# Attention scores as pairs of 64-row products, the first batch's values as pairs of 64-column products, and q and k without copies

## The chip, the cores and the metric

The kernel runs on one core of a Trainium2 chip. The metric is device time in microseconds (us) of one execution: the median of three runs before the change is 488.28 us (487.72 to 488.59).

## The reference, cut to what matters

Attention with a narrow local window and a few global keys, on 4 batches of 8 heads, 768 tokens and 64 values per head, is followed by a gated feed-forward block that mixes over tokens. Inputs and output are float32.

```python
scores = q @ k.T / 8 - slope[h] * dist          # per batch and head
keep   = (col < 8) | ((row - col >= 0) & (row - col < 96))
a      = softmax(where(keep, scores, -1e9))
x      = concat_heads(a @ v)                     # [4, 768, 512]
h      = relu(x @ w_in)                          # [4, 768, 1024]
u, vv  = h[..., :512], layer_norm(h[..., 512:])
out    = (u * (w_spatial @ vv + b)) @ w_out      # [4, 768, 512]
```

## The kernel before, in words

**Tiles.** The work is cut into 24 tiles of 128 tokens, six to a batch (n = 0 to 23, i = n mod 6). A query tile needs only its own block of 128 keys and the one before it, with the global keys copied over the first 32 columns of the older block. So the scores of a head are 128 rows by W columns, with W = 128 for i = 0 and 256 otherwise. `scores(n)` (line 942) makes them, adds the bias, takes the exponential and normalises. `values(n)` (line 1016) transposes them and multiplies with v. `mlp_v`, `mlp_u`, `mlp_s` and `mlp_o` (lines 1105 to 1181; V, U, G and O in the plan) are the feed-forward block; `setup_w_in`, `setup_w_out` and `setup_w_t` (I, Q and T, lines 815 to 828) split the weights into a high and a low part.

**Two ways of multiplying.** In the first batch (n < 6) q, k, v and the probabilities stay float32 (`whole_s`, `whole_v`); the trace shows each such product as two matrix instructions on TensorE (PE). In the other batches each operand is split into a high and a low part of a shorter format (fp32r) and one product is one instruction per pair of parts.

**Scores.** The array has 128 rows and one head fills 64. In the first batch q is stored twice with the other head's half zeroed (memsets at line 865), so that a product with all 128 rows of k gives one head (line 975): 8 products a tile. In the other batches q's high part is stored on both halves, and so is its low part; k's high part lies on the rows 0 to 63 and its low part on the rows 64 to 127. Two products of 128 rows (line 978) then sum all four pairs of parts: 16 products a tile. `split_qk` and `prep_k` (lines 891 to 905) load a block as `raw`, write the high part to `rawh` (ScalarE, ACT, mostly) and the low part back into `raw` (VectorE, DVE), and DMAs on SyncE's queue (SP) copy both into place: 8 of 128 KB for q (lines 879 to 882) and 4 for k. One pair of heads uses one PSUM bank.

**Values of the first batch.** v is stored with zero blocks between the heads (`padded`, line 926), so that a product of 128 columns fills the rows of one head and adds zero to the other's (lines 1049 to 1054): 16 products a tile, 8 for n = 0.

**Order.** All operations are first recorded (`Recorder`, line 89). `plan` (line 348) then simulates five queues with the durations of `cost` (line 223) and, for each engine, takes the ready operation of lowest rank; the ranks are the step's due time plus an offset in KEYS (line 534). Six PSUM banks are shared by scores (tag s), transposes (p), the feed-forward block (m) and the weights (cv); `room` (line 387) gives a bank to a new tile, and two more banks hold the results of `values`. `keep_warm` (line 505) puts spare transposes of the identity into gaps of PE in the first stretch. All operations are issued from line 39, which is why the profile shows that line everywhere.

Of the kernel before, what the change touches and what calls it, by code (L numbers as in the profile page):

```python
# [10 lines left out]
F32 = mybir.dt.float32  # L11
# [15 lines left out]
CFG = {'WS': 6, 'WV': 6, 'kept': 'p', 'bias1': 'pppppppp', 'bias2': 'a', 'S': [['I01', 'A'], ['I00', 'T00', 'T01', 'A', 'V00', 'B00'], ['T02', 'T03', 'A', 'V01', 'U00'], ['T04', 'T05', 'A', 'V02'], ['Q00', 'Q01', 'A', 'V03', 'U01'], ['Q02', 'Q03', 'A', 'V04']], 'T': [['V15', 'U12', 'A'], ['G10', 'O10', 'A'], ['G11', 'O11', 'A'], ['G12', 'O12', 'V00', 'V01', 'U00', 'A'], ['V02', 'A'], ['V03', 'U01', 'A', 'V04']], 'END': ['V05', 'U02', 'G00', 'O00', 'G01', 'O01', 'G02', 'O02'], 'whi': 'aaax', 'wsub': 'xx', 'wadd': 'v', 'wth': 'a', 'wtl': 'p', 'vhi': 'p', 'vlo': 'p', 'qhi': 'xv', 'qlo': 'v', 'khi': 'a', 'klo': 'v', 'pth0': 'a', 'x0h': 'x', 'x0l': 'v', 'pth': 'a', 'xh': 'aa', 'c1': 'a', 'xl': 'vppv', 'vnh': 'xvpa', 'vnl': 'p', 'gm': 'x', 'gh': 'aa', 'gl': 'x', 'o': 'vava', 'norm0': 'p', 'norm': 'p', 'wp': 3, 'wc': 'v', 'we': 'p',  'vrn': 'v', 'dup': 1, 'fold': '', 'xb': 1, 'div': 'v', 'rows': 'a', 'xf0h': 'aa', 'xf0l': 'pppp', 'xdiv': 'v', 'xbh': 'a', 'xbl': 'p', 'b_rawqk': 1, 'b_ev': 3, 'b_raw': 1, 'b_pr': 10, 'b_pth': 2, 'b_c1': 3, 'b_ps_s': 2, 'b_ps_p': 2, 'b_ps_o': 2, 'b_ps_m': 2}  # L27
# [3 lines left out]
class Op:  # L31
# [6 lines left out]
    def issue(self):  # L38
        getattr(self.real, self.call)(*[placed(x) for x in self.args], **{n: placed(x) for n, x in self.kw.items()})  # L39
# [49 lines left out]
class Recorder:  # L89
# [21 lines left out]

    def add(self, engine, call, args, kw):
        op = Op()
        op.ways = ((engine, call, args, kw),)
        op.token = self.now
        op.take(0)
        outs = [kw[x] for x in ("out", "accum_out") if x in kw]
        ins = [x for n, x in kw.items() if n not in ("out", "accum_out") and isinstance(x, (bass.AP, Ref))]
        aps = [x for x in args if isinstance(x, (bass.AP, Ref))]
        if "out" not in kw:  # L120
            outs.insert(0, aps.pop(0))
        op.writes, op.reads = outs, ins + aps
        op.num = len(self.ops)
        op.holds = list(dict.fromkeys(x.tile for x in outs + ins + aps if isinstance(x, Ref)))
        for v in op.holds:
            v.ops.append(op)
        self.ops.append(op)
# [95 lines left out]
def cost(op):  # L223

    out = op.writes[0]
    n = elements(out)
    src = op.reads[0] if op.reads else out
    psum = any(in_psum(x) for x in op.reads + op.writes[:1])
    parts = list(out.ap)[0][1]
    if op.eng == "tensor":  # L230
        if op.call == "transpose":
            return 109, 0, False
        n = elements(op.kw["rhs"])
        if op.kw["rhs"].dtype == F32:
# [24 lines left out]
    if op.call == "tensor_scalar" and not one and isinstance(op.kw.get("scalar1"), bass.AP) and n > 256:  # L259
        return 75 + .85 * n, 0, True  # L260
    if op.call in ("tensor_scalar", "tensor_copy") and not one:
        return (75 + 1.04 * n if out.dtype == I32 else 70 + .53 * n), 0, True
    if op.call in ("tensor_reduce", "bn_stats"):
        return 70 + 1.04 * elements(src), 0, False
    if op.call == "bn_aggr":
        return 180, 0, False
    return (190 if parts < P else 74) + 1.04 * n + (0 if one else 60), 0, not one


def link(ops):  # L270

    wrote, used, bank, forms = {}, {}, {}, {}
    for op in ops:
        preds = set()
        for ap in op.reads:
            name, p0, p1, bits = extent(ap)
            for q0, q1, b, o in wrote.get(name, ()):
                if q0 < p1 and p0 < q1 and b & bits:
                    preds.add(o)
        op.after = set(preds)  # L280
        for ap in op.reads + op.writes:

            own = ap.tile.name if isinstance(ap, Ref) else ap.tensor.name
            if own in places:
                mine = forms.setdefault(places[own], {})
                mine.setdefault(own, set()).add(op.num)
                for other in mine:
                    if other != own:
                        preds |= mine[other]
        for ap in op.writes:  # L290
            name, p0, p1, bits = extent(ap)
            for table in (wrote, used):
                for q0, q1, b, o in table.get(name, ()):
                    if q0 < p1 and p0 < q1 and b & bits:
                        preds.add(o)
        for ap in op.reads:
            name, p0, p1, bits = extent(ap)
            used.setdefault(name, []).append((p0, p1, bits, op.num))
        for ap in op.writes:
            name, p0, p1, bits = extent(ap)  # L300
            for table in (wrote, used):
                if name in table:
                    table[name] = [x for x in table[name] if not (p0 <= x[0] and x[1] <= p1 and x[2] | bits == bits)]
            wrote.setdefault(name, []).append((p0, p1, bits, op.num))
        if op.eng == "tensor":
            name = extent(op.writes[0])
            half = name[0], name[3].bit_length() > 1024
            if half in bank:
                preds.add(bank[half])
            bank[half] = op.num  # L310
# [22 lines left out]
def gates(ops):  # L333
# [3 lines left out]
    for v in {v: None for op in ops for v in op.holds}:  # L337
# [3 lines left out]
        if v.tag in IN_TURN:  # L341
            if v.tag in before:
                found.append((before[v.tag], first.num))
            before[v.tag] = first.num
# [3 lines left out]
def plan(ops, keys, trace=None):  # L348
# [38 lines left out]
    def room(x, e):  # L387

        v = ops[x].holds[0] if ops[x].holds else None
        if v is None or v.place is not None:  # L390
            return 0.0, None
        if len(banks) - 1 < sum(KEEP.get(tag, 0) for tag in FLOAT if tag != v.tag and not held[tag]):
            return None, None
        best = None
        for b, last in banks.items():
            at = max((reach(o, ops[x], e, ends[o.num], stands[o.num]) for o in last), default=0.0)
            if best is None or at < best[0]:
                best = at, b
        return best or (None, None)

    done = 0
    while done < n:
# [69 lines left out]
        done += 1  # L472
        for v in op.holds:
            if v.place is None:
                v.place = bank
                del banks[bank]
                held[v.tag] += 1
# [54 lines left out]
SLACK = 120  # L532
DMA_FIRST, DMA_PRE, DMA_POST, DMA_MARGIN = 4200.0, 800.0, 1400.0, 800.0
# [4 lines left out]
def attn_then_spatial_gating_kernel(  # L538
# [403 lines left out]
    def scores(n, qq):  # L942
# [25 lines left out]
        for g in range(NP):  # L968
            if g == 2:
                yield  # L970
# [398 lines left out]
```

## Time and profile before

| | |
|---|---|
| median of three runs | 488.28 us |
| the profiled execution's own time | 489.19 us |
| its span, first to last instruction | 487.4 us |
| granted clock of PE, mean | 0.998 |
| DMA traffic | 65.50 MB |

PE is TensorE's products, PEld its weight loads, DVE VectorE, ACT ScalarE, POOL GpSimd and SPq the queue of SyncE, which issues the DMAs. Products are pipelined: the duration of one is longer than the step from one to the next, so a step is read from the starts of two lines of the timeline, divided by the count of the first. Tiles are named by the program: `bank` is one of the six PSUM banks, `kring` and `q` are the operands of the scores, `ops` is the result of `values`, `vring` holds v, `pr` the probabilities, `pth` their transposes.

### The profile page before, as it was taken

What the parts mean: (1) busy time and instruction counts of PE and PEld (TensorE: products, weight loads), DVE (VectorE), ACT (ScalarE), POOL (GpSimd) and SP (SyncE); (2) the same over time, 40 slices, a digit from 0 to 9 for tenths busy, and PEclk for the clock granted to TensorE, in tenths of its full rate; (3) what the DMA queues carried; (4) which work ended last, traced back from release to release, by engine and by line L of the source; (5) the groups of instructions that cost most, each with busy time, mean ns of one, the idle gap of its engine ahead of it and who ended that gap; (6) DMA issues with size and microseconds to landing.
All of it is one profiled execution on the core that took longest, in us unless ns stands there. A gap on an engine that the chain in (4) does not pass through costs nothing.

```text
span 487.4 us, 10076 instructions
## 1 busy us (share of the span) xinstructions
PE 465.8 (96%) x3286; PEld 430.0 (88%) x3286; DVE 355.7 (73%) x1021; ACT 285.6 (59%) x773; POOL 267.4 (55%) x419
## 2 busy tenths in 40 slices
PE   7989999998999999899999999998989999999996
PEld 7778889998988779889999998998979998899995
DVE  3999788957686798798886787766766878762532
ACT  1899877653675577785745675665556576630112
POOL 4779897782363676687535263784243763543000
PEclk9999999999999999999999999999999999999999
DMA  6946634365645776665725552762564860000012
GB/s 208 319 155 179 179 114 114 99 155 141 154 116 164 204 191 176 169 166 139 199 68 150 153 151 86 197 173 66 133 154 118 220 166 25 34 1 3 22 45 71
DMA packets 38028, 65.50 MB, mean 134 GB/s; under 512 B 6000, under 2 KB 9840, under 8 KB 37968
## 3 DMA queue, kind: packets, MB, share of 16 engines
q1 hardware_dynamic: 37968, 64.77, 48.5%
q8 instruction: 28, 0.46, 0.4%
q14 instruction: 32, 0.26, 0.2%
HBM read 29.76 MB, written 6.68 MB: 75 GB/s over the span
## 4 chain that ended last, share of the span: by engine, by line
PE 60%; DMA 12%; DVE 10%; ACT 8%; issue 4%; SPq 3%; POOL 2%; DVEq 0%; ACTq 0%; POOLq 0%
PE bank L39 54%; PE ops L39 6%; ACT pr L39 4%; SPq L39 3%; DMA kring<-raw 3%; DVE pr L39 2%; DVE c L39 2%; DMA q<-raw 2%; DMA kring<-in_k_dram 2%; DMA raw<-in_k_dram 2%; DMA gl<-in_moe_w_spatial_dram 1%; DMA raw<-in_q_dram 1%; DVE bank L39 1%; ACT pth L39 1%; DMA gh<-in_moe_w_spatial_dram 1%
## 5 line engine op out<-in xcount | busy, mean ns | idle before, releaser
L39 POOL TENSOR_SCALAR pr<-pr,rc 128x256 f32<-128x256 f32 (+1 forms) x192 | 93.3, 504 | 27.4 <-DVE rc L39 13.9
L39 ACT ACTIVATE pr<-pr,mn 128x256 f32<-128x256 f32 (+1 forms) x192 | 92.1, 482 | 18.9 <-DVE mn L39 18.3
L39 DVE CUSTOM_DVE_ANT_0 pr<-bank,bias 128x256 f32<-128x256 f32 (+1 forms) x192 | 68.2, 396 | 12.5 <-PE bank L39 11.1
L39 PE MATMUL bank<-kring,q 128*128 128x256 f32 (+1 forms) x384 | 65.2, 304 | 6.2 <-DMA kring<-raw 2.1
L39 DVE TENSOR_TENSOR c<-ops,c 64x256 f32<-64x256 f32 x144 | 60.5, 420 | 12.7 <-ACT c L39 9.4
L39 PE MATMUL ops<-pth,vring 128*128 128x256 f32 (+1 forms) x440 | 63.2, 282 | 3.9 <-DVE c L39 2.4
L39 ACT ACTIVATE pth<-bank 128x512 fp32r<-128x512 f32 (+3 forms) x96 | 51.4, 556 | 24.7 <-PE bank L39 16.8
L39 PEld LDWEIGHTS ops<-pth,vring 128*128 128x128 f32 x440 | 57.3, 190 | 8.0 <-ACT pth L39 2.7
L39 PEld LDWEIGHTS bank<-kring,q 128*128 128x128 f32 x384 | 54.6, 189 | 10.9 <-ACT pth L39 1.8
L39 PE MATMUL bank<-ident,pr 128*128 128x128 f32 x352 | 60.5, 274 | 3.0 <-POOL pr L39 2.6
L39 POOL TENSOR_TENSOR xtl<-c,xth 128x256 fp32r<-128x256 f32 x36 | 28.5, 793 | 53.9 <-ACT xth L39 44.9
L39 DVE TENSOR_TENSOR pth<-bank,pth 128x512 fp32r<-128x512 f32 (+1 forms) x72 | 45.1, 641 | 16.1 <-ACT pth L39 15.2
L39 PEld LDWEIGHTS bank<-ident,pr 128*128 128x128 f32 x352 | 42.3, 140 | 9.4 <-POOL pr L39 5.0
L39 PE MATMUL bank<-w_t_l,vnh 128*128 128x256 f32 x288 | 46.6, 286 | 0.0
L39 PE MATMUL bank<-w_t_h,vnl 128*128 128x256 f32 x288 | 46.0, 285 | 0.0
L39 PE MATMUL bank<-w_t_h,vnh 128*128 128x256 f32 x288 | 45.1, 284 | 0.0
L39 ACT ACTIVATE rawh<-raw 128x512 fp32r<-128x512 f32 x29 | 18.3, 630 | 37.0 <-DMA raw<-in_k_dram 21.5
L39 PEld LDWEIGHTS bank<-w_t_l,vnh 128*128 128x128 f32 x288 | 39.1, 189 | 0.1
L39 PEld LDWEIGHTS bank<-w_t_h,vnh 128*128 128x128 f32 x288 | 38.8, 189 | 0.5
L39 PEld LDWEIGHTS bank<-w_t_h,vnl 128*128 128x128 f32 x288 | 38.9, 189 | 0.1
L39 POOL TENSOR_TENSOR vnl<-ev,vnh 128x512 fp32r<-128x512 f32 x24 | 31.5, 1314 | 10.7 <-DVE vnh L39 4.3
L39 ACT ACTIVATE gh<-ev 128x512 fp32r<-128x512 f32 x24 | 15.1, 629 | 37.0 <-DVE ev L39 18.2
(105 smaller groups left out, 987.2 us busy)
## 6 DMA issues: line engine op xcount, KB each, us to landing
q<-rawh SPq DMA_DIRECT2D x72, 128.0 KB, 2.4
q<-raw SPq DMA_DIRECT2D x72, 128.0 KB, 2.4
out_dram<-ev SPq DMA_DIRECT2D x23, 256.0 KB, 2.4
raw<-in_q_dram SPq DMA_DIRECT2D x18, 256.0 KB, 3.0
raw<-in_v_dram SPq DMA_DIRECT2D x18, 256.0 KB, 2.9
raw<-in_k_dram SPq DMA_DIRECT2D x18, 256.0 KB, 2.8
kring<-rawh SPq DMA_DIRECT2D x36, 128.0 KB, 2.9
kring<-raw SPq DMA_DIRECT2D x36, 128.0 KB, 2.4
```

Source lines behind the costliest of these rows:

```text
L39: getattr(self.real, self.call)(*[placed(x) for x in self.args], **{n: placed(x) for n, x in self.kw.items()})
```

## The change

Scores: for each head the product takes only its 64 rows of q and k. The products of the two heads of a pair stand one after the other in the stream, on different halves of the array's rows and with different PSUM banks as their targets. In the first batch this is one product per head; in the other batches three (high by high, high by low, low by high; low by low is left out). Two pairs of heads (`SG` = 2 in CFG; four pairs for i = 0) form one recorded operation, `halves64`, whose products follow one another without others between: 12 for fp32r with W = 256, 24 for i = 0, and 4 or 8 in the first batch. It takes two banks at once.

Values of the first batch: each head's product takes its 64 columns of v and writes its half of the PSUM rows; two pairs of heads form one operation of 8 products (4 for n = 0). v lies without zero blocks.

Preparation: q and k are split from `raw` straight into the tiles from which the products read, so the 12 copying DMAs of a tile go, as do the memsets; q has two tiles in turn, and the loads take `raw` and `rawh` in turn.

The planner gives a `halves64` operation a cost of SWITCH = 180 ns plus a cost per pair, hands out several banks at once, and has new offsets in KEYS. The diff, without the lines of CFG and KEYS and the dependency bookkeeping:

```diff
@@ -36,6 +36,10 @@
         self.eng, self.real = engine.name, engine.real
 
     def issue(self):
+        if self.call == "halves64":
+            for kw in self.args:
+                self.real.matmul(**{n: placed(x) for n, x in kw.items()})
+            return
         getattr(self.real, self.call)(*[placed(x) for x in self.args], **{n: placed(x) for n, x in self.kw.items()})
 
...
@@ -108,6 +112,14 @@
             return getattr(engine, call)(*args, **kw)
         self.add(*ways[0])
         self.ops[-1].ways = ways
+
+    def halves64(self, parts):
+
+        if not self.open:
+            for kw in parts:
...
@@ -230,6 +245,9 @@
     if op.eng == "tensor":
         if op.call == "transpose":
             return 109, 0, False
+        if op.call == "halves64":
+            n = elements(op.args[0]["rhs"])
+            return SWITCH + len(op.args) // 2 * (max(216, 4 * n * .422) if op.args[0]["rhs"].dtype == F32 else max(107, n * .461)), 0, False
...
@@ -386,17 +405,15 @@
 
     def room(x, e):
 
-        v = ops[x].holds[0] if ops[x].holds else None
-        if v is None or v.place is not None:
-            return 0.0, None
-        if len(banks) - 1 < sum(KEEP.get(tag, 0) for tag in FLOAT if tag != v.tag and not held[tag]):
+        new = [v for v in ops[x].holds if v.place is None]
+        if not new:
+            return 0.0, ()
+        if len(banks) - len(new) < sum(KEEP.get(tag, 0) for tag in FLOAT if tag != new[0].tag and not held[tag]):
             return None, None
-        best = None
-        for b, last in banks.items():
-            at = max((reach(o, ops[x], e, ends[o.num], stands[o.num]) for o in last), default=0.0)
-            if best is None or at < best[0]:
-                best = at, b
-        return best or (None, None)
+        found = sorted((max((reach(o, ops[x], e, ends[o.num], stands[o.num]) for o in last), default=0.0), b) for b, last in banks.items())
+        if len(found) < len(new):
+            return None, None
+        return found[len(new) - 1][0], [b for _, b in found[:len(new)]]
 
     done = 0
...
@@ -860,58 +879,44 @@
         if whole_s(n):
             if n == 0:
                 for x in range(2):
-                    t = ring["q", x] = work.tile([P, 2, NP, P], F32, name="q0", tag=f"q{x}", bufs=1)
-                    for j, s_ in enumerate(halves):
-                        nc.gpsimd.memset(t[halves[1 - j], j], 0.0)
+                    ring["q", x] = work.tile([P, NP, P], F32, name="q0", tag=f"q{x}", bufs=1)
                 ring["k"] = work.tile([P, 3, NP, P], F32, name="kring0", tag="kring", bufs=1)
-            q1 = ring["q", n % 2]
-            for j, s_ in enumerate(halves):
-                nc.sync.dma_start(out=q1[s_, j], in_=q[b, i, j])
+            qt = ring["q", n % 2]
+            nc.sync.dma_start(out=qt, in_=block(q, b, i))
             nc.sync.dma_start(out=ring["k"][:, n % 3], in_=block(k, b, i))
-            return q1, None
+            return qt
         if n == CFG["WS"]:
+            for x in range(2):
+                ring["q", x] = work.tile([P, 2, NP, P], F32R, name="q1", tag=f"q{x}", bufs=1)
             ring["k"] = work.tile([P, 2, 2, NP, P], F32R, name="kring", tag="kring", bufs=1)
             if i:
-                prep_k(n - 1, [(0, slice(0, NGMAX)), (i - 1, slice(NGMAX, P))])
-        q1 = work.tile([P, 2, NP, P], F32R, name="q1", tag="q0", bufs=1)
-        ql = work.tile([P, 2, NP, P], F32R, name="ql", tag="q1", bufs=1)
-        parts = split_qk(0, q, b, [(i, slice(0, P))])
-        for j, s_ in enumerate(halves):
-            for o_ in halves:
-                for dst, part in zip((q1, ql), parts):
-                    nc.sync.dma_start(out=dst[o_, j].bitcast(F32), in_=part[s_].bitcast(F32))
-        prep_k(n, [(i, slice(0, P))])
-        return q1, ql
+                split_k(n - 1, [(0, slice(0, NGMAX)), (i - 1, slice(NGMAX, P))])
+        qt = ring["q", n % 2]
+        split_qk(0, n, q, [(i, slice(0, P))], qt)
+        split_k(n, [(i, slice(0, P))])
+        return qt
 
     halves = [slice(64 * j, 64 * j + 64) for j in range(2)]
 
     def block(src, b, i):
         return src[b, i].rearrange("two d g x -> (two d) g x")
 
-    def split_qk(x, src, b, pieces):
-        raw = work.tile([P, NP, P], F32, name="qkraw", tag=f"raw{x}", bufs=1)
-        hi = work.tile([P, NP, P], F32R, name="qkhi", tag=f"rawh{x}", bufs=1)
+    def split_qk(x, n, src, pieces, dst):
+        raw = work.tile([P, NP, P], F32, name="qkraw", tag=("raw", "rawh")[n % 2] + str(x), bufs=1)
         for i, cols in pieces:
-            nc.sync.dma_start(out=raw[:, :, cols], in_=block(src, b, i)[:, :, cols])
-        lo = raw.bitcast(F32R)
-        hi_lo(raw, hi, lo, E(("qhi", "khi")[x]), E(("qlo", "klo")[x]))
-        return hi, lo
-
-    def prep_k(n, pieces):
-        kc = ring["k"][:, n % 2]
-        parts = split_qk(1, k, n // NB, pieces)
-        for j, s_ in enumerate(halves):
-            for part, o_ in zip(parts, halves):
-                nc.sync.dma_start(out=kc[o_, j].bitcast(F32), in_=part[s_].bitcast(F32))
+            nc.sync.dma_start(out=raw[:, :, cols], in_=block(src, n // NB, i)[:, :, cols])
+        hi_lo(raw, dst[:, 0], dst[:, 1], E(("qhi", "khi")[x]), E(("qlo", "klo")[x]))
+
+    def split_k(n, pieces):
+        split_qk(1, n, k, pieces, ring["k"][:, n % 2])
 
     def prep_v(n):
         b, i = divmod(n, NB)
         rows = v[b, i * P:(i + 1) * P, :]
...
@@ -923,9 +928,6 @@
             vg[b] = dram.tile([NGMAX, 2 * DM], F32, name="vg")
             nc.sync.dma_start(out=vg[b], in_=vr[0:NGMAX].bitcast(F32).rearrange("p g x d -> p (g x d)"))
 
-    def padded(slot, part):
-        return ring["v", True][part, slot, 0:3 * NP].rearrange("p (g x) d -> p g x d", x=3)[:, :, 1:3]
-
     def split_v(n, pieces):
         raw = work.tile([P, DM], F32, name="raw", tag="raw", bufs=nb("raw"))
         for i, rows in pieces:
...
@@ -965,24 +966,29 @@
         rc = work.tile([P, H], F32, name="rc", bufs=2)
         W = P if i == 0 else 2 * P
         probs = held[n] = []
-        for g in range(NP):
-            if g == 2:
+        passes = ((0, 0),) if whole_s(n) else ((0, 0), (0, 1), (1, 0))
+        size = NP if i == 0 else CFG["SG"]
+        per = min(size, 512 // W)
+        for g in range(1, NP, 2):
+            if g == 3:
                 yield
-            sp = ps_s.tile([P, 2, W], F32, name="sp", tag="s")
-            for j in range(2):
-                h = 2 * g + j
-                if whole_s(n):
-                    nc.tensor.matmul(sp[:, j], lhsT=q1[:, j, g], rhs=kring[:, sl, g], start=True, stop=True)
-                    continue
-                for y, a in enumerate((q1, ql)):
-                    nc.tensor.matmul(sp[:, j], lhsT=a[:, j, g], rhs=kring[:, sl, j, g], start=(y == 0), stop=(y == 1))
-            for j in range(2):
-                h = 2 * g + j
+            if (g - 1) % size == 0:
+                sps = [[ps_s.tile([P, per, W], F32, name="sp", tag="s") for j in range(2)] for _ in range(size // per)]
+                parts = []
+                for f in range(g - 1, g - 1 + size):
+                    pair = sps[(f - g + 1) // per]
+                    for y, (x, z) in enumerate(passes):
+                        for sp, s_ in zip(pair, halves):
+                            a, b_ = (qt[s_, f], kring[s_, sl, f]) if whole_s(n) else (qt[s_, x, f], kring[s_, sl, z, f])
+                            parts.append(dict(out=sp[:, f % per], lhsT=a, rhs=b_, start=(y == 0), stop=(y == len(passes) - 1)))
+                nc.halves64(parts)
+            for h in range(2 * g - 2, 2 * g + 2):
+                sp = sps[h // 2 % size // per][h % 2]
                 pr = work.tile([P, W], F32, name="pr", bufs=nb("pr"))
                 probs.append(pr)
                 bt = bias0[:, h] if i == 0 else bias[:, h, off:off + W]
                 nc.vector.tensor_tensor_reduce(
-                    out=pr, in0=sp[:, j], in1=bt, scale=-scale, scalar=3e38, op0=ALU.add, op1=ALU.min,
+                    out=pr, in0=sp[:, h // 2 % per], in1=bt, scale=-scale, scalar=3e38, op0=ALU.add, op1=ALU.min,
                     accum_out=mn[:, h:h + 1],
                 )
                 nc.scalar.activation(pr, pr, AF.Exp, bias=mn[:, h:h + 1], scale=-1.0, accum_out=sm[:, h, 0:1])
@@ -1045,20 +1051,22 @@
                 pth = work.tile([P, nch, 2 * P], F32, name="pth0", tag="pth", bufs=nb("pth"))
                 ptf = pt.rearrange("p c j x -> p c (j x)")
                 cp(E("pth0", g), pth, ptf)
-                ops = opsring[:, n % 2].rearrange("p two x -> p (two x)").rearrange("p (g x) -> p g x", x=P)
-                for y in range(2 * nch):
-                    c, j = divmod(y, 2)
-                    nc.tensor.matmul(
-                        ops[:, g], lhsT=vring[:, order[c], 3 * g + 2 - 2 * j:3 * g + 4 - 2 * j].rearrange("p x d -> p (x d)"), rhs=pth[:, c, j * P:(j + 1) * P],
-                        start=(y == 0), stop=(y == 2 * nch - 1),
-                    )
+                ops = opsring[:, g // 2].rearrange("p two x -> p (two x)")[:, 0:2 * P].rearrange("p (g x) -> p g x", x=P)
+                vals = vring.rearrange("p s (g two d) -> p s g two d", two=2, d=D)
+                if g % 2 == 0:
+                    parts = []
+                for c in range(nch):
+                    for j, s_ in enumerate(halves):
+                        parts.append(dict(out=ops[s_, g % 2], lhsT=vals[:, order[c], g, 1 - j], rhs=pth[:, c, j * P:(j + 1) * P], start=(c == 0), stop=(c == nch - 1)))
+                if g % 2:
+                    nc.halves64(parts)
                 if g % 2:
                     if folded(n):
                         xs = work.tile([P, 2, P], F32, name="xs", tag="c1", bufs=nb("c1"))
-                        nc.vector.tensor_tensor(out=xs, in0=ops[:, gs], in1=div[:, gs], op=ALU.mult)
+                        nc.vector.tensor_tensor(out=xs, in0=ops, in1=div[:, gs], op=ALU.mult)
                         hi_lo(xs, xh[:, gs, toks], xl[:, gs, toks], E("xf0h", g // 2), E("xf0l", g // 2))
                     else:
-                        hi_lo(ops[:, gs], xh[:, gs, toks], xl[:, gs, toks], E("x0h", g // 2), E("x0l", g // 2))
+                        hi_lo(ops, xh[:, gs, toks], xl[:, gs, toks], E("x0h", g // 2), E("x0l", g // 2))
                 continue
             pth = work.tile([P, 2 * nch, 2, P], F32R, name="pth", bufs=nb("pth"))
             hi_lo(pt.rearrange("p c j x -> p (c j) x"), pth[:, :, 0], pth[:, :, 1], E("pth", g), nc.vector)
...
@@ -1094,7 +1102,7 @@
             two(E("xl", g), xl[:, g, toks], c1, c2, ALU.add)
         if 1 <= i < NB - 1:
             if whole_v(n):
-                nc.sync.dma_start(out=padded(n % 3, slice(0, NGMAX)), in_=v[b, 0:NGMAX, :])
+                nc.sync.dma_start(out=vring[0:NGMAX, n % 3], in_=v[b, 0:NGMAX, :])
             else:
                 nc.sync.dma_start(out=vring[0:NGMAX, n % 3].bitcast(F32).rearrange("p g x d -> p (g x d)"), in_=vg[b])
         yield
```

## Rows read from the trace of the kernel before

**Rows 1.** The page, busy time of each engine over the span.
```profile
PE 465.8 (96%) x3286; PEld 430.0 (88%) x3286; DVE 355.7 (73%) x1021; ACT 285.6 (59%) x773; POOL 267.4 (55%) x419
```

**Rows 2.** Five stretches: length, then each engine's busy us, PE's clock, DMA.
```profile
0.00:16.00 16.00, 12.96 (x98) 12.96 (x99) 7.36 (x54) 5.74 (x22) 5.63 (x17) 1.00 0.75 224
16.00:60.00 44.00, 41.00 (x259) 34.67 (x257) 40.28 (x134) 40.45 (x117) 39.03 (x64) 1.00 0.70 207
60.00:110.00 50.00, 49.83 (x366) 47.01 (x367) 40.35 (x104) 33.40 (x80) 41.55 (x60) 1.00 0.42 119
110.00:420.00 310.00, 299.20 (x2139) 277.34 (x2138) 238.71 (x682) 191.74 (x531) 167.32 (x263) 1.00 0.55 146
420.00:490.00 70.00, 62.80 (x432) 57.97 (x430) 29.04 (x49) 14.28 (x28) 13.84 (x19) 0.97 0.07 25
```

**Rows 3.** The chain that ended last, pieces in order: start, us, what.
```profile
8.30 8.96 DMA kring<-in_k_dram
...
17.28 4.90 DMA gh<-in_moe_w_spatial_dram
...
115.06 2.96 DMA kring<-raw
...
221.01 3.66 DMA q<-raw
```

**Rows 4.** PE timeline, first batch: start, us, operation, count.
```profile
11.27 1.95 PE L39 MATMUL bank<-kring,q 128*128 128x128 f32 x16
13.06 1.15 PE L39 MATMUL bank<-ident 128*128 128x128 f32 x9
...
28.55 2.05 PE L39 MATMUL ops<-pth,vring 128*128 128x128 f32 x16
30.44 0.82 PE L39 MATMUL bank<-ident,pr 128*128 128x128 f32 x6
...
35.27 1.89 PE L39 MATMUL bank<-kring,q 128*128 128x256 f32 x8
37.00 0.60 PE L39 MATMUL bank<-ident,pr 128*128 128x128 f32 x4
```

**Rows 5.** PE timeline, fp32r products of 512, 128 and 256 columns.
```profile
97.77 1.09 PE L39 MATMUL bank<-w_in_h,xth 128*128 128x512 f32 x4
98.70 1.07 PE L39 MATMUL bank<-w_in_l,xth 128*128 128x512 f32 x4
...
102.89 1.90 PE L39 MATMUL bank<-kring,q 128*128 128x128 f32 x16
104.63 0.56 PE L39 MATMUL bank<-w_t_h,vnh 128*128 128x256 f32 x3
...
118.59 0.87 PE L39 MATMUL bank<-kring,q 128*128 128x256 f32 x6
119.31 0.40 PE L39 MATMUL ops<-pth,vring 128*128 128x256 f32 x2
```

**Rows 6.** PE groups from 110 us on, and weight loads of the scores.
```profile
L39 PE MATMUL bank<-kring,q 128*128 128x256 f32 x240 | 36.4, 285 | 3.9 <-DMA kring<-raw 2.1 <-ACT pth L39 1.3 <-DVE mn L39 0.5
...
L39 PEld LDWEIGHTS bank<-kring,q 128*128 128x128 f32 x384 | 54.6, 189 | 10.9 <-ACT pth L39 1.8 <-issue 1.7 <-DVE w_in_l L39 1.2
```

**Rows 7.** Products that write ops (values), 16 to 110 us, by stretch.
```profile
16.00:60.00 44.00, 13.69 (x105) 12.77 (x105) 3.75 (x9) 1.92 (x5) 1.00 0.70 207
60.00:110.00 50.00, 8.99 (x72) 8.62 (x72) 3.33 (x8) 0.77 (x2) 1.00 0.42 119
```

**Rows 8.** Products that read kring (scores), 16 to 60 us.
```profile
16.00:60.00 44.00, 16.43 (x64) 11.20 (x64) 0.90 (x3) 1.00 0.70 207
```

**Rows 9.** The copies of q and k on SP, and the last weights' split.
```profile
L39 SPq DMA_DIRECT2D q<-rawh x72: 461/587/612, 52.5 to 393.0; - x72
...
L39 SPq DMA_DIRECT2D kring<-raw x36: 461/588/873, 98.6 to 399.8; - x36
...
L39 DVE TENSOR_TENSOR w_in_l<-bank,ev x8: 660/680/689, 23.0 to 70.0; 128x512 fp32r<-128x512 f32 x8
```

**Rows 10.** What PE waited for, 110 to 420 us: total, times, longest.
```profile
PE ops L39 <- DVE c L39: 2.4, 3, 2.1
PE bank L39 <- DMA kring<-raw: 2.1, 2, 1.6
```

More of the change, by code (lines that the diff above doesn't have):

```diff
@@ L25 @@
 NGMAX = 32
[L27 removed]
+CFG = {'WS': 6, 'SG': 2, 'WV': 6, 'kept': 'p', 'bias1': 'pppppppp', 'bias2': 'a', 'S': [['I01', 'A'], ['I00', 'T00', 'T01', 'A', 'V00', 'B00'], ['T02', 'T03', 'A', 'V01', 'U00'], ['T04', 'T05', 'A', 'V02'], ['Q00', 'Q01', 'A', 'V03', 'U01'], ['Q02', 'Q03', 'A', 'V04']], 'T': [['V15', 'U12', 'A'], ['G10', 'O10', 'A'], ['G11', 'O11', 'A'], ['G12', 'O12', 'V00', 'V01', 'U00', 'A'], ['V02', 'A'], ['V03', 'U01', 'A', 'V04']], 'END': ['V05', 'U02', 'G00', 'O00', 'G01', 'O01', 'G02', 'O02'], 'whi': 'aaax', 'wsub': 'xx', 'wadd': 'v', 'wth': 'a', 'wtl': 'p', 'vhi': 'p', 'vlo': 'p', 'qhi': 'xv', 'qlo': 'v', 'khi': 'a', 'klo': 'v', 'pth0': 'a', 'x0h': 'x', 'x0l': 'v', 'pth': 'a', 'xh': 'aa', 'c1': 'a', 'xl': 'vppv', 'vnh': 'xvpa', 'vnl': 'p', 'gm': 'x', 'gh': 'aa', 'gl': 'x', 'o': 'vava', 'norm0': 'p', 'norm': 'p', 'wp': 3, 'wc': 'v', 'we': 'p',  'vrn': 'v', 'dup': 1, 'fold': '', 'xb': 1, 'div': 'v', 'rows': 'a', 'xf0h': 'aa', 'xf0l': 'pppp', 'xdiv': 'v', 'xbh': 'a', 'xbl': 'p', 'b_rawqk': 1, 'b_ev': 3, 'b_raw': 1, 'b_pr': 10, 'b_pth': 2, 'b_c1': 3, 'b_ps_s': 2, 'b_ps_p': 2, 'b_ps_o': 2, 'b_ps_m': 2}
 NLMAX = 97
@@ L110, in either @@
         self.ops[-1].ways = ways
+    def halves64(self, parts):
+        if not self.open:
+            for kw in parts:
+                self.tensor.matmul(**kw)
+            return
+        self.add(self.tensor, "halves64", parts, {})
     def add(self, engine, call, args, kw):
@@ L119, in add @@
         aps = [x for x in args if isinstance(x, (bass.AP, Ref))]
-        if "out" not in kw:
+        if call == "halves64":
+            outs = [x["out"] for x in args]
+            ins = [x[n] for x in args for n in ("lhsT", "rhs")]
+        elif "out" not in kw:
             outs.insert(0, aps.pop(0))
@@ L305, in link @@
         if op.eng == "tensor":
[L306 to L310, printed above, removed]
+            for ap in op.writes:
+                name = extent(ap)
+                half = name[0], name[3].bit_length() > 1024
+                if half in bank:
+                    preds.add(bank[half])
+                bank[half] = op.num
         preds.discard(op.num)
@@ L341, in gates @@
         if v.tag in IN_TURN:
-            if v.tag in before:
+            if before.get(v.tag, first.num) != first.num:
                 found.append((before[v.tag], first.num))
@@ L472, in plan @@
         done += 1
+        bank = list(bank)
         for v in op.holds:
             if v.place is None:
-                v.place = bank
-                del banks[bank]
+                v.place = bank.pop(0)
+                del banks[v.place]
                 held[v.tag] += 1
@@ L532 @@
 SLACK = 120
+SWITCH = 180.0
 DMA_FIRST, DMA_PRE, DMA_POST, DMA_MARGIN = 4200.0, 800.0, 1400.0, 800.0
[L534 removed]
@@ L911, in prep_v @@
             if n == 0:
-                t = ring["v", True] = work.tile([P, 3, 3 * NP + 1, D], F32, name="vring0", tag="vring", bufs=1)
-                nc.gpsimd.memset(t[:, :, 0::3], 0.0)
-            nc.sync.dma_start(out=padded(n % 3, slice(0, P)), in_=rows)
+                ring["v", True] = work.tile([P, 3, DM], F32, name="vring0", tag="vring", bufs=1)
+            nc.sync.dma_start(out=ring["v", True][:, n % 3], in_=rows)
             return
@@ L940, in attn_then_spatial_gating_kernel, with scores @@
     held = {}
-    def scores(n, qq):
-        q1, ql = qq
+    def scores(n, qt):
         b, i = divmod(n, NB)
@@ L952, in globs @@
                 return kring[:, x, :, 0:NGMAX]
-            return kring[:, x].rearrange("p j g x -> p (j g) x")[:, :, 0:NGMAX].bitcast(F32)
+            return kring[:, x].rearrange("p y g x -> p (y g) x")[:, :, 0:NGMAX].bitcast(F32)
         if i == 0:
```

2 lines of the change are left out of this document (1 added, 1 removed).

## The prediction

> **What bounds the kernel now.** I read the busy shares first: TensorE (PE) has 465.8 us of products in a span of 487.4, the next engine 355.7 [rows 1]. A busy PE need not be a PE at its limit, so the second view is the table of stretches [rows 2]. From 60 us on PE is full: 49.83 of 50 us, then 299.20 of 310, the clock granted at its upper level of 2.4 GHz (1.00). From 16 to 60 us PE has 41.00 of 44, but VectorE (DVE) has 40.28, ScalarE (ACT) 40.45 and GpSimd (POOL) 39.03: four engines share the bound there, because the weights are split beside the attention of the first batch. Third, the chain [rows 3]: up to 22 us it hangs on loads of k and of weights, and after 110 us it passes now and then through a copy of k or q. So PE time saved before 16 us is worth nothing, between 16 and 60 us little, and after 60 us nearly all.
>
> **Prices of a product.** Steps are differences of starts in the timeline. A float32 product is two instructions. Scores with 256 columns: (37.00-35.27)/8 = 0.216 us an instruction; values with 128 columns: (30.44-28.55)/16 = 0.118; scores of tile 0: (13.06-11.27)/16 = 0.112 [rows 4]. For fp32r, 256 columns step by (119.31-118.59)/6 = 0.120, 128 columns by (104.63-102.89)/16 = 0.109, and 512 columns by (98.70-97.77)/4 = 0.232 [rows 5]. From 512 to 256 columns the step halves; from 256 to 128 it hardly moves. So something that does not go with the columns takes 0.109, and I read it as the weight load, one for each product.
>
> **What is unknown.** No product on half of the rows or columns is in this trace, so two prices are bounded. First, a pair of halves: at best it costs what one full product costs now (0.120 for fp32r with 256 columns, 0.109 with 128), at worst its two weight loads follow each other, 2 x 0.109 = 0.218. I take the lower one: loads of different rows of the array need not wait for each other, and the rows show that loads hide behind products already. Second, the change of shape before and after a group: nothing at best; at worst the pipe empties twice, each time the 0.285 of one product less its step 0.120 = 0.165, and one weight load of 0.189 stands free [rows 6], together 0.52. I take 0.17 for a group, one emptying.
>
> The Trainium skill has a rule on either side. TensorE: Matmul & The Clock Gate, section LDWEIGHTS, says that a load's time goes with its columns and not with its rows, so a load for 64 rows is not cheaper; the flat step of rows 5 agrees. TensorEngine Tiling (Array Packing), Tiling Modes, says that different tiles can run loads and products in parallel and that a change of mode drains the engine; no run here shows either yet. By the first alone the pair costs 0.218, which is rival 1; by the second it costs 0.120.
>
> **The sum on PE, part by part.**
> - Scores, first batch: tile 0 goes from 16 x 0.112 = 1.79 to 8 x 0.112 + 0.17 = 1.07. The ten groups of tiles 1 to 5 go from 8 x 0.216 = 1.73 to 4 x 0.216 + 0.17 = 1.03, 0.70 each, 7.0 in all.
> - Values, first batch: ten groups from 16 x 0.118 = 1.89 to 8 x 0.118 + 0.17 = 1.11, 0.78 each, 7.8; tile 0's two groups 0.30 each, 0.6.
> - Scores, later batches: 30 groups from 8 x 0.120 = 0.96 to 6 x 0.120 + 0.17 = 0.89, 0.07 each, 2.1; three tiles with i = 0 from 16 x 0.109 = 1.74 to 12 x 0.109 + 0.17 = 1.48, 0.8 in all.
>
> That is 0.7 + 7.0 + 8.4 + 2.9 = 19.0 us of PE. Not all of it reaches the end.
> - Tile 0's scores run at 11 us among spare transposes [rows 4], in the stretch that waits for loads: 0.
> - From 16 to 60 us lie 64 of the 80 score instructions [rows 8], 8 groups, 5.6 us, and 105 instructions of the values [rows 7], tile 0 and some 5.5 groups, 4.9 us. These 10.5 us lie beside DVE and ACT at 92%; packed without a gap their 40.4 us leave at most 3.5 of the 44. The U products also wait for the last split of w_in, which DVE begins at 70.0 [rows 9]. I take 2 us for the stretch itself and 2.5 for one V block of 12 products of 512 columns (12 x 0.232 = 2.8) that PE can do earlier: 4.5.
> - From 60 to 110 us lie 2 groups of scores and 4.5 of values: 4.9 us, with PE full. DVE (40.35) and POOL (41.55) still fit into 45. I take 4.
> - The 2.9 of the later batches count in full.
>
> **Copies.** 12 copying DMAs of each of 18 tiles go, 216 of some 0.59 us on SP's queue [rows 9], 7 us a tile. SP is no bound; they cost only where a tile's scores wait for them: PE lost 2.1 us to kring<-raw directly [rows 10], and the chain shows pieces of 3 to 4 us [rows 3] whose delay comes back in other waits. PE is idle for 310 - 299.2 = 10.8 us of that stretch [rows 2]. I take 2.5, between the 2.1 and the 10.8. Splitting work on ACT and DVE stays the same in size. Fewer memsets on POOL before 16 us: 0, loads cover them. Fewer loads of q (6) at the start: 0, the bytes are the same.
>
> **Added waits.** The split of k(n) now writes the slot that scores(n-1) read; it waits for PE on ACT instead of on SP. Behind it on ACT are exponentials that need those scores too, so little is held up. A group wants two banks of six and all its inputs at once, and a values group waits for the transposes of both pairs: late next is the DVE read of the first scores, by half a group, 0.4 us, which PE covers with feed-forward products after 60 us. In the first stretch this cover is thin; up to 23 groups (11 of scores, 12 of values) of 0.4 us, 9 us, would be lost if there were none. Taken as 0, kept for the range. New offsets reorder everything; 0, between nothing in either direction and a few us.
>
> **Sum.** 4.5 + 4 + 2.9 + 2.5 = 13.9 us. The profiled execution took 489.19 us, 0.9 above the median of 488.28; 489.19 - 13.9 = 475.3, which against the median is 474.4. I predict **474.5 us**.
>
> **Rivals.**
> 1. *Weight loads in turn (slower).* If a fp32r pair costs 0.218, a group of 12 costs 6 x 0.218 + 0.17 = 1.48 instead of 0.96, 15.6 us over 30 groups, and the i = 0 tiles 12 x 0.218 + 0.17 = 2.79 instead of 1.74, 3.1 over three. The first batch keeps its gain: a group of four float32 scores has 8 loads, 0.87 us, as long as its columns take (4 x 0.216), and I let a load of half the columns take half the time. So 2.9 turns into -18.7, and 4.5 + 4 + 2.5 - 18.7 = -7.7: about 496 us, 490 to 501. It decides from 0.18 a pair on, where the 216 pairs of the later batches, 0.06 to 0.07 dearer, eat the 13.9 us. For it: the flat 0.109. Against it: only that loads overlap products today. Chance 0.11.
> 2. *The other engines bound the whole first batch.* Its PE gain is lost in waits for DVE, ACT and POOL, and only 2.9 + 2.5 and a little more are left: 479 to 487, at 483. For it: 92% in rows 2. Against it: from 60 us on PE alone is full. Chance 0.18.
> 3. *Everything counts.* The planner refills PE, the 18.3 after 16 us count and half of the 10.8 idle goes: 489.19 - 0.9 - 24 = 464 to 469. Chance 0.17.
> 4. *The pairs gain nothing.* The change of shape costs 0.52 instead of 0.17: 0.35 more for 56 groups, 19.6 us, takes the whole sum of PE, and the time stays: within 0.2%, 487.3 to 489.3. Chance 0.04.
>
> The forecast, 469 to 479, has 0.50. **How the numbers follow.** Faster by over 0.2% (about 1 us, what a measurement can tell) are the forecast and rivals 2 and 3: 0.85; same 0.04; slower 0.11. The range takes the forecast, rival 3 but for its end and rival 2 nearly whole: 465 to 486 leaves out some 0.2.
>
> **What would show it.** Right: score products with 64 rows whose pairs step by about 0.120 with 256 columns; a gap of about 0.17 around a group; no q<-raw and kring<-raw; PE busy some 15 to 20 us lower, with more idle PE before 60 us than the 3 now; values of the first batch over by 85 us instead of 91. Wrong: pairs that step by 0.2 (rival 1), gaps of 0.5 (rival 4), PE still short of work at 100 us (rival 2), or as little idle PE before 60 us as now (rival 3).

## The result and the profile after

The changed kernel takes **476.46 us** (median of 4 runs, 475.69 to 477.20) against 488.43 us of the kernel before beside it: ratio 0.9747, 95% interval 0.971 to 0.9784. 474.5 was predicted, 465 to 486 as the range. The number was right, but by luck: three terms of its sum were wrong, and their errors cancel.

The page of the changed kernel: span, busy time of each engine, DMA traffic, and the chain by engine. The copies of q and k are gone (65.50 MB of traffic became 37.16), and the chain that ended last, which had DMAs in it, is 88% PE.

```profile
span 474.2 us, 9947 instructions
PE 460.5 (97%) x3470; PEld 408.9 (86%) x3470; DVE 354.3 (75%) x1019; ACT 283.8 (60%) x771; POOL 264.0 (56%) x418
DMA packets 17962, 37.16 MB, mean 78 GB/s; under 512 B 2448, under 2 KB 2704, under 8 KB 17904
PE 88%; DVE 5%; ACT 3%; issue 1%; DMA 1%; POOL 0%; DVEq 0%; ACTq 0%; POOLq 0%
```

The stretches of the changed kernel, which answer to [rows 2] (length, busy us of PE, PEld, DVE, ACT, POOL, clock, DMA):

```profile
0.00:16.00 16.00, 14.29 (x114) 14.01 (x115) 8.07 (x57) 6.03 (x23) 3.02 (x12) 1.00 0.76 270
16.00:60.00 44.00, 38.94 (x290) 26.50 (x287) 42.12 (x128) 40.58 (x110) 39.28 (x66) 1.00 0.55 184
60.00:110.00 50.00, 49.27 (x412) 44.34 (x409) 41.69 (x112) 33.88 (x88) 41.86 (x57) 1.00 0.32 96
110.00:420.00 310.00, 308.87 (x2311) 278.05 (x2311) 243.04 (x693) 194.87 (x538) 172.31 (x275) 1.00 0.19 59
420.00:490.00 70.00, 49.13 (x354) 46.03 (x352) 19.35 (x32) 8.48 (x15) 7.57 (x11) 0.99 0.07 24
```

From 110 to 420 us PE is idle for 310 - 308.87 = 1.1 us; before it was 10.8 [rows 2]. From 16 to 60 us it idles more than before, 5.1 instead of 3.0 us, with DVE at 42.12 of 44.

The timeline of PE in the changed kernel (start, us, operation, count): a group of 12 fp32r score products between full products, the 24 of a tile with i = 0, and float32 groups of values and of scores in the first batch.

```profile
112.20 0.52 PE L43 MATMUL bank<-w_t_h,vnh 128*128 128x256 f32 x3
112.65 0.97 PE L41 MATMUL bank<-kring,q 64*128 64x256 f32 x12
113.56 0.39 PE L43 MATMUL bank<-w_t_l,vnh 128*128 128x256 f32 x1
113.78 0.40 PE L43 MATMUL ops<-pth,vring 128*128 128x256 f32 x2
...
97.70 0.64 PE L43 MATMUL bank<-xth,w_in_l 128*128 128x256 f32 x4
98.27 1.55 PE L41 MATMUL bank<-kring,q 64*128 64x128 f32 x24
99.75 0.51 PE L43 MATMUL bank<-w_t_h,vnh 128*128 128x256 f32 x2
...
40.78 0.39 PE L43 MATMUL bank<-w_in_l,xth 128*128 128x512 f32 x1
41.10 1.09 PE L41 MATMUL ops<-pth,vring 128*64 128x128 f32 x16
42.13 0.96 PE L43 MATMUL bank<-w_in_l,xth 128*128 128x512 f32 x3
43.02 1.13 PE L41 MATMUL bank<-kring,q 64*128 64x256 f32 x8
44.08 1.20 PE L43 MATMUL bank<-w_in_h,xtl 128*128 128x512 f32 x4
45.21 0.49 PE L41 MATMUL bank<-kring,q 64*128 64x256 f32 x2
```

Read the first four lines with the full step of 0.120. The group takes 113.56 - 112.65 = 0.91. It begins late by 112.65 - 112.20 - 3 x 0.12 = 0.09, and the full product after it steps by 0.22 instead of 0.12, 0.10 more. Together **1.10 us**, against 0.96 for the 8 products before (8 x 0.120 [rows 5]): the group became dearer. The 24 take 1.48 + 0.09 + 0.10 = 1.67, against 1.74. With the same 0.2 at the ends, the values' group takes 1.03 + 0.2 = 1.23 against 1.89, and the float32 scores 1.06 + 0.2 = 1.26 against 1.73 [rows 4].

Weight loads of the changed kernel, mean ns of one behind the comma:

```profile
L41 PEld LDWEIGHTS bank<-kring,q 64*128 64x128 f32 x528 | 35.8, 186 | 11.1 <-issue 3.6 <-DVE mn L43 1.4 <-ACT pth L43 0.8
...
L41 PEld LDWEIGHTS ops<-pth,vring 128*64 128x64 f32 x176 | 9.4, 136 | 4.4 <-ACT pth L43 2.1 <-issue 1.5 <-DVE xtl L43 0.3
```

A load of 64 rows is as long as one of 128 (186 against 189 ns [rows 6]); one of 64 columns is shorter (136 ns, though not half). The Trainium skill, TensorE: Matmul & The Clock Gate, section LDWEIGHTS, says that a load's time goes with its columns and not with its rows; the trace agrees. The loads of [rows 5], with which the prediction compared this rule, belong to products of the full array and could not show it.

Last, the spare transposes that fill gaps of PE in the first stretch, in the kernel before and in the changed one:

```profile
L39 PE MATMUL bank<-ident 128*128 128x128 f32 x82 | 11.5, 311 | 3.0 <-POOL ident masks.py:199 3.0
```

```profile
L43 PE MATMUL bank<-ident 128*128 128x128 f32 x122 | 16.6, 301 | 1.7 <-POOL ident masks.py:199 1.7
```

They count as busy and compute nothing that is used: 5.1 us more of them after the change are 5.1 us more of hidden gap.

### The profile page after: what moved, and what is told of

It reads as the page before. It is cut to its first block, busy times and chain, and to the rows that moved or that the text cites. A ratio compares the mean times of both kernels' runs of the same rounds, so it can differ in the third digit from the quotient of the medians.

```text
span 474.2 us, 9947 instructions
## 1 busy us (share of the span) xinstructions
PE 460.5 (97%) x3470; PEld 408.9 (86%) x3470; DVE 354.3 (75%) x1019; ACT 283.8 (60%) x771; POOL 264.0 (56%) x418
## 2 busy tenths in 40 slices
DMA packets 17962, 37.16 MB, mean 78 GB/s; under 512 B 2448, under 2 KB 2704, under 8 KB 17904
## 4 chain that ended last, share of the span: by engine, by line
PE 88%; DVE 5%; ACT 3%; issue 1%; DMA 1%; POOL 0%; DVEq 0%; ACTq 0%; POOLq 0%
PE bank L43 73%; PE bank L41 7%; PE ops L43 7%; DVE bank L43 2%; PE ops L41 1%; DVE pr L43 1%; ACT pr L43 1%; ACT ev L43 1%; DMA q<-in_q_dram 1%; ACT w_in_h L43 1%; ACT pth L43 0%; DVE w_in_l L43 0%; POOL ev L43 0%; DVE raw L43 0%; DVE rawh L43 0%
## 5 line engine op out<-in xcount | busy, mean ns | idle before, releaser
L43 POOL TENSOR_SCALAR pr<-pr,rc 128x256 f32<-128x256 f32 (+1 forms) x192 | 89.8, 484 | 43.5 <-DVE rc L43 36.7
L41 PE MATMUL bank<-kring,q 64*128 64x256 f32 (+1 forms) x528 | 47.3, 308 | 0.5 <-DVE mn L43 0.3
L41 PEld LDWEIGHTS bank<-kring,q 64*128 64x128 f32 x528 | 35.8, 186 | 11.1 <-issue 3.6
L43 PE MATMUL bank<-w_t_l,vnh 128*128 128x256 f32 x288 | 45.0, 285 | 0.0
L43 PE MATMUL ops<-pth,vring 128*128 128x256 f32 x264 | 41.5, 289 | 0.0
L43 ACT ACTIVATE ev<-bank 128x512 f32<-128x512 f32 (+1 forms) x37 | 21.5, 583 | 33.0 <-PE bank L43 27.0
L43 PEld LDWEIGHTS ops<-pth,vring 128*128 128x128 f32 x264 | 35.6, 190 | 1.7 <-DVE pth L43 0.2
```

What stands on the lines that cost most here:

```text
L41: self.real.matmul(**{n: placed(x) for n, x in kw.items()})
```

## The experiments

| run | what it is | us | ratio to before, 95% |
|---|---|---|---|
| changed kernel | | 476.46 | 0.9747 (0.971 to 0.9784) |
| e1 | changed, old offsets | 515.79 | 1.0551 (1.0498 to 1.0605) |
| e2 | before, new offsets | 541.10 | 1.1083 (1.1005 to 1.1161) |
| e3 | first batch only, new offsets | 536.00 | 1.0988 (1.093 to 1.1045) |
| e4 | later batches only, new offsets | 498.00 | 1.0175 (1.011 to 1.024) |
| n1 | before, no offsets | 516.75 | 1.0588 (1.0536 to 1.064) |
| n2 | changed, no offsets | 496.80 | 1.0181 (1.0135 to 1.0227) |
| f1 | low by low put back, same order | 483.44 | 0.9909 (0.987 to 0.9949) |
| f2 | parts copied again, same order | 618.73 | 1.2709 (1.2631 to 1.2787) |
| t1 | first batch only, refitted | 487.88 | 0.998 (0.9947 to 1.0014) |
| t2 | later batches only, refitted | 482.37 | 0.9869 (0.9837 to 0.9901) |
| t3 | SWITCH = 400, refitted | 479.83 | 0.9811 (0.978 to 0.9842) |
| t4 | SG = 4, SWITCH = 400, refitted | 485.15 | 0.9919 (0.9887 to 0.9951) |

### Offsets swapped, and one half of the change at a time

```diff
 e1: after.py
-KEYS = {'start': -325.0164,
+KEYS = {'start': -148.4611,
...
 e2: before.py
-KEYS = {'start': -148.4611,
+KEYS = {'start': -325.0164,
...
```

> The changed kernel with the plan's offsets (KEYS) of the kernel before. Theory A (structure): what the changed trace gained, 9.7 us less idle PE from 110 to 420 us and about 4.6 us of lead when the first batch ends, comes from the products and from the missing copies, and the offsets only fit the plan to them: 476 to 481 us. Rival B (offsets): the new offsets refill PE: 483 to 490 us.

> The kernel before with the offsets of the changed kernel. Theory A: no gain, 488 to 493 us, the copies still make PE wait about 10 us after 110 us. Rival B: 478 to 484 us, and idle PE after 110 us falls to a few us.

Both theories missed. Each kernel with the other's offsets is slower than with its own by 39.3 us (515.79 - 476.46) and 53 us (541.10 - 487.96), so neither set is better; each fits one list of operations. These runs cannot say what the structure is worth.

The two halves of the change, each with the new offsets:

```diff
 e3: scores(n), from the second batch on as before
+        if not whole_s(n):
+            q1, ql = qt
...
+                for j in range(2):
+                    for y, a in enumerate((q1, ql)):
+                        nc.tensor.matmul(sp[:, j], lhsT=a[:, j, g], rhs=kring[:, sl, j, g], start=(y == 0), stop=(y == 1))
...
 e4: scores(n) and values(n), first batch as before
+        if whole_s(n):
...
+                    nc.tensor.matmul(sp[:, j], lhsT=qt[:, j, g], rhs=kring[:, sl, g], start=True, stop=True)
...
```

> Halves in the first batch alone; from the second batch on the scores are products of 128 rows with copied operands, as before. Theory A: only the lead of the first batch is left, 4 to 5 us: 483 to 485 us, and PE idles some 10 us from 110 to 420. Rival C (the prediction's sum): the first batch is worth 8.5 us: about 480.

> Halves and no copies from the second batch on; the first batch's scores and values are products of 128 rows and 128 columns, as before. Theory A: the idle PE after 110 us goes (-9.7) and each of 30 groups costs 0.13 us more than the 8 products before (+4): 482 to 484 us. Rival C: 2.9 + 2.5 us: about 483, but with PE time falling and not the idle time.

Missed too, for the same reason: with offsets made for another list, e3 (536.0) lies near e2. With the new offsets, the kernel before, e3, e4 and the changed kernel take 541.1, 536.0, 498.0 and 476.5. This says how near each list lies to the one that the offsets were made for, and at most hints that the later batches' part weighs more.

### No offsets at all

```diff
-KEYS = {'start': -325.0164,
...
+KEYS = {}
```

> The kernel before with no offsets at all (KEYS empty): the plan goes by due times alone. The swapped offsets cost 28 to 53 us, so each set fits one kernel only, and no swapped run weighs the structure. Without offsets both kernels stand on equal ground: theory A (structure) says this one is 8 to 20 us slower than the changed kernel without offsets; rival B (offsets) says the two lie within 4 us. Level: 515 to 535 us.

> The changed kernel with no offsets at all. Theory A: 8 to 20 us faster than the kernel before without offsets; rival B: within 4 us of it. Level: 500 to 515 us.

The stretch from 110 to 420 us of n1, then of n2:

```profile
110.00:420.00 310.00, 297.85 (x2063) 273.90 (x2062) 232.36 (x631) 178.80 (x482) 165.56 (x256) 0.97 0.52 140
```

```profile
110.00:420.00 310.00, 303.33 (x2261) 274.98 (x2260) 231.60 (x667) 181.08 (x508) 174.51 (x270) 0.99 0.18 57
```

Without offsets the changed kernel is 20 us faster (516.75 - 496.80), at the edge of what theory A expected, and its idle time in this stretch is 6.7 against 12.2 us; at 496.80 it lies below the 500 to 515 expected for it. Theory B, within 4 us, does not fit, and a gain of the structure does. But each run is one unfitted plan, the swapped offsets moved such plans by 39 and 53 us, and the mean granted clock differs too (0.967 for n1, 0.981 for n2), so 20 us is no measure of the structure.

### What a pair costs, in the same order

```diff
-        passes = ((0, 0),) if whole_s(n) else ((0, 0), (0, 1), (1, 0))
+        passes = ((0, 0),) if whole_s(n) else ((0, 0), (0, 1), (1, 0), (1, 1))
```

The fourth product is issued but not shown to the planner, so the order of everything else stays.

> The changed kernel with the low by low products put back, 8 pairs a group instead of 6 from the second batch on; the order of all instructions is that of the changed kernel. If PE is the bound after the first batch and a pair costs 0.12 us (0.109 with 128 columns), 30 x 0.24 + 3 x 0.44 = 8.5 us: 485 us. If two loads in turn set the pair (0.218): +16, 492. If PE has room: under 480.

PE timeline of this run, groups of 16 and of 32:

```profile
112.17 1.21 PE L41 MATMUL bank<-kring,q 64*128 64x256 f32 x16
113.31 0.38 PE L43 MATMUL bank<-w_t_l,vnh 128*128 128x256 f32 x1
...
97.34 2.00 PE L41 MATMUL bank<-kring,q 64*128 64x128 f32 x32
99.27 1.57 PE L43 MATMUL bank<-w_t_h,vnh 128*128 128x256 f32 x11
```

Two more pairs lengthen the group from 0.91 to 1.14: **0.115 us a pair**; four more with 128 columns from 1.48 to 1.93: 0.1125. So the two halves run beside each other, loads included, and rival 1 of the prediction (0.218) falls. The Trainium skill, TensorEngine Tiling (Array Packing), says so under Tiling Modes, and the trace agrees. What is left of a group of 12 is 1.10 - 6 x 0.115 = **0.41 us for the change of shape**, in and out; of the 24 with 128 columns, 1.67 - 12 x 0.1125 = 0.32. By these rows the run should be 30 x 0.23 + 3 x 0.45 = 8.3 us longer. It is 7.0 (483.44 - 476.46), or some 7.9 by the two ratios, each to the kernel before beside it (0.9909 and 0.9747): after the first batch nearly every microsecond of PE counts. The run also says what the low by low product is worth: 7 to 8 of the 12 us hang on leaving it out, and a group with all four products, 8 x 0.115 + 0.41 = 1.33 us, is far dearer than the 0.96 before.

### The copies put back, in the same order

```diff
+            for part in again.get((self.writes[0].tensor.name, self.writes[0].offset), ()):
+                Op.sp.dma_start(out=part, in_=part)
```

> The changed kernel, same order of all its instructions, but after the split each part of q and k from the second batch on is copied onto itself by DMAs, 12 of 128 KB a tile as before the change, and the scores wait for them. Theory A: the copies' waits come back, 5 to 12 us, 481 to 488, as idle PE between 110 and 420 us. Rival: DMAs have room and loads come early, within 2 us: 475 to 478.

What PE waited for longest in this run:

```profile
PE bank L50 <- DMA kring<-kring: 36.3, 19, 4.8
PE bank L52 <- DVE mn L52: 11.1, 5, 3.5
```

One of the waits of SP's queue in this run:

```profile
SPq L46 <- DMA q<-q: 48.0, 45, 4.1
```

The stretch from 110 to 420 us:

```profile
110.00:420.00 310.00, 246.51 (x1600) 216.76 (x1600) 172.20 (x507) 139.73 (x392) 122.26 (x196) 0.87 0.47 115
```

The run is 142 us slower than the changed kernel, over ten times what was expected, and so no measure of the copies in the kernel before, whose plan left them room. Part of it is of the run's own making: to come to 8 copies, each part of q is copied onto itself twice, and SP waits 48.0 us for such copies of q to land. What it does show: 12 copies a tile that the order does not allow for stand in SP's queue ahead of the loads and make PE wait. With the waits the granted clock is lower (0.87 in this stretch against 1.00), and the same products take 518.4 us of PE instead of 460.5.

### One half of the change at a time, refitted

e3 and e4 again, with offsets searched for each on its own plan.

> Halves in the first batch alone, later batches with 128-row products and copies as before; offsets refitted to this kernel by a search on its own plan. Theory A: the first batch's lead without the rest, 4 to 6 us below the kernel before: 482 to 485, and PE still idles 7 to 12 us from 110 to 420 us. Theory D (offsets): a good fit alone closes the gaps: 476 to 479, idle under 3 us.

> Halves without copies from the second batch on, the first batch with 128 rows and 128 columns as before; offsets refitted in the same way. Theory A: gaps from 110 to 420 us gone (-10 to -12), shape changes of 30 groups added (+4): 480 to 483, idle under 3 us. Theory D: 476 to 479 as well as the kernel above. If copies were worth only the prediction's 2.5 us: 486 to 490.

The same stretch of t1, then of t2, and the chain of t1 by line:

```profile
110.00:420.00 310.00, 301.36 (x2141) 278.22 (x2140) 238.88 (x691) 190.57 (x531) 170.28 (x266) 1.00 0.54 144
```

```profile
110.00:420.00 310.00, 308.59 (x2329) 279.84 (x2329) 235.93 (x670) 192.08 (x525) 170.26 (x266) 1.00 0.19 58
```

```profile
by line: PE bank L43 53.1%; PE ops L43 4.9%; ACT pr L43 3.6%; DMA raw<-in_k_dram 3.5%; DMA kring<-raw 2.9%; issue 2.8%; DVE pr L43 2.5%; DMA q<-raw 2.4%; DVE bank L43 2.4%; SPq L43 2.3%; DVE c L43 1.5%; DVE raw L43 1.3%; DMA kring<-rawh 1.1
```

t2 came as theory A said: 482.4, idle 1.4 us. t1 did not: its idle time is as expected (8.6 us), its time is not. It cannot be told from the kernel before (0.998). It begins the scores of the second batch at 98.97 us, 3.9 earlier than before, and by the end this lead is 3.0 us by span and 1.2 by median. But where these scores begin is also a choice of the plan: t2, whose first batch is as before, begins them at 94.06.

```profile
94.06 1.56 PE L41 MATMUL bank<-kring,q 64*128 64x128 f32 x24
```

Safer is what PE has left at 110 us. The products other than scores that start later, at the steps of [rows 5], come to 327.5 us before, 322.7 in the changed kernel and 325.4 in t1, by an estimate from the traces, with the same tiles' scores left in all three: leads of 4.9 and 2.1 us. Against the product of the two ratios, 0.998 x 0.9869 = 0.985, both halves together give 0.9747, some 5 us more: their gains do not simply add. Either the first batch's gain counts only when the later batches are free of gaps, or this refit made less of it to begin with (2.1 of 4.9); how good each refit is, is not known, and the runs do not decide it. Theory D finds no support: this refit with copies leaves 8.6 us of gaps.

### Two attempts at a better version

```diff
 t3 and t4
-SWITCH = 180.0
+SWITCH = 400.0
...
 t4 alone
-CFG = {'WS': 6, 'SG': 2,
+CFG = {'WS': 6, 'SG': 4,
...
```

> The changed kernel with SWITCH = 400 in the planner's cost, what the trace shows for a group's change of shape (0.40 us) instead of 180, and offsets refitted to it. A plan that knows the price should lose less to it: 471 to 475 us. If the price is already hidden by the order: 475.5 to 478.

> As the one before (SWITCH = 400, refitted), but SG = 4: the four pairs of heads of a tile follow one another, one change of shape a tile instead of two, in four banks instead of two. 15 changes of 0.40 us fewer are 6 us of PE: 469 to 472 if nothing else moves. Rival: four of six banks at once make transposes and feed-forward products wait for banks: 478 to 486, with idle PE after 110 us.

t3 is slower than the changed kernel (479.83 against 476.46, though the intervals of the two ratios just overlap), so a truer price alone did not help; whether a longer search for its offsets would, stays open. t4, its group of a tile in the timeline, its spare transposes, its stretch from 16 to 110 us and its longest wait:

```profile
117.05 1.70 PE L41 MATMUL bank<-kring,q 64*128 64x256 f32 x24
118.67 0.98 PE L43 MATMUL bank<-w_t_h,vnh 128*128 128x256 f32 x6
```

```profile
L43 PE MATMUL bank<-ident 128*128 128x128 f32 x241 | 32.4, 301 | 1.7 <-POOL ident masks.py:199 1.7
```

```profile
16.00:110.00 94.00, 85.42 (x693) 72.31 (x692) 80.94 (x235) 70.11 (x188) 73.17 (x112) 0.95 0.40 130
PE bank L43 <- POOL pr L43: 5.6, 3, 4.3
```

The group is as cheap as hoped: 1.62 + 0.2 = 1.82 us a tile against 2 x 1.10. After 110 us PE has as few gaps as in the changed kernel (308.98 of 310). But the gaps ahead of it grew: 32.4 us of spare transposes against 16.6, and 8.6 us idle from 16 to 110 us against 5.8. The granted clock is 0.95 in that stretch, where the changed kernel has 1.00: by an estimate up to 94 x 0.05 = 4.7 of the 8.7 us lost. The rival was right about the time and wrong about the place, and its cause, banks, is not shown: the longest wait is for the probabilities that POOL normalises. No version beat the changed kernel.

## Why the prediction was right, and where its terms were wrong

**The bound.** PE after 60 us, four engines before it: right. f1 shows the first (7.0 of 8.3 us count); the changed kernel's DVE at 42.12 of 44 us, with PE idle for 5.1, speaks for the second.

**The price of a pair.** Taken as 0.120, measured 0.115: right; the lower bound was the one.

**The change of shape.** "I take 0.17 for a group, one emptying": this step failed in size. Measured 0.41 with 256 columns, near the upper bound of 0.52, and 0.32 with 128. By the measured groups PE gains some 12 us in the first batch and loses 4.0 in the later ones, 8 where the sum had 19.0: 11 us less. The later batches' groups, forecast at -0.07 each, came at +0.14: 30 x 0.14 = 4.2 us lost, less 0.2 for the i = 0 tiles, where 2.9 were to be won. The planner's 180 ns was too low as well.

**The first batch.** By the steps above, ten groups of scores save 0.47 each and ten of values 0.66, 11.3 us, with tile 0 some 12, where the prediction had 16. To 110 us the idle time and the spare transposes together are 17.7 us before (6.2 + 11.5) and 24.1 after (7.5 + 16.6): 6.4 us of the 12 became gaps. The scores of the second batch begin at 98.27 instead of 102.89 [rows 5], a lead of 4.6 us (4.9 by the products left at 110 us); 8.5 were forecast for this stretch. That only a part of PE's gain would come out was right, for the reason given: PE idles more beside a DVE that is nearly full.

**The copies.** "I take 2.5, between the 2.1 and the 10.8": failed in size, on the other side. PE's idle time from 110 to 420 us fell by 9.7 us. The wait named after the copies was 2.1 us [rows 10], but the chains show what a wait list does not. In the kernel before, the copy that starts at 115.06 and takes 2.96 us [rows 3] is followed by

```profile
118.03 2.58 DMA raw<-in_k_dram
120.68 0.63 ACT rawh L39
```

The next load into `raw` starts when the copy out of it has landed, and the next split waits for that load; the chain of t1 has the same pairs, and the delay ends as a wait for DVE or POOL. Shown is that the later batches' part, halves without copies, closes the gaps (t1 against t2). That it is the copies in it and not the grouping of products is argued from the chains and from f2. Nor is it shown that it is the copies themselves: the change also lets the loads take `raw` and `rawh` in turn, and a kernel with copies but a second tile to load into, planned for, was not tried.

**The sum.** Forecast 4.5 + 4 + 2.9 + 2.5 = 13.9. Found by span (487.4 - 474.2 = 13.2): 4.6 of lead from the first batch, -4.0 for the later groups, 9.7 of idle time, and 2.9 beyond these. Each gap follows a product whose tail of 0.165 counts as busy, and from 110 to 420 us PE waits 2 times instead of 15, so fewer gaps explain some 13 x 0.165 = 2.1 of it, by an estimate. The errors, -3.9 in the first batch, -6.9 in the later groups, +7.2 for the copies and +2.9, cancel to -0.7; that is luck.

**The marks.** PE busy was to fall by 15 to 20 us: it fell by 5.3, and by 10.4 without the spare transposes. A gap of 0.17 around a group: 0.41, nearer to the 0.5 named as a sign against. Values of the first batch over by 85 us: 89.6 (88.57 + 1.03). More idle PE before 60 us: right, 5.1 against 3.0 from 16 us on. Three of the marks said that the reasons were off while the number held.

## What to carry to other kernels

In this kernel two half products beside each other cost what one full product costs, but entering and leaving the half shape costs as much as three or four fp32r products of 256 columns (0.41 against 0.120): group them, and count what the group replaces. A stage whose products got cheaper by 12 us gave 4.6 here, where other engines fill it; whether such a lead reaches the end with gaps behind it, t1 leaves open. And a plan fitted to a list of operations has to be fitted again before any part of a change is weighed: the swapped offsets cost more than the whole gain.

## What the runs showed that was not expected

- A change of the array's shape: 0.41 us for a group of 12 fp32r products with 256 columns, about the same for one of 24 (1.82 - 12 x 0.115 = 0.44), and 0.32 for one of 24 with 128 columns.
- The list of waits names 2.1 us of PE's idle time after the copies; 9.7 us went with the part of the change that took them out.
- Gaps are paid twice. e1 has the list of operations of the changed kernel, and its span is 40.6 us longer. PE idles 19.0 us more (32.7 against 13.7) and has 7.3 more of spare transposes (23.9 against 16.6); the other 14.3 are the products themselves, 458.2 us instead of 443.9, at a mean granted clock of 0.971 instead of 1.000.
